# Memory branch: two heads share one score tile in 64-row halves, values in 64-column tiles, and TensorE's order is a fixed list

## The chip, the cores and the metric

The kernel runs on one core of one Trainium2 chip. The metric is the device time of one launch in microseconds (us); lower is better. Before the change it is 3423.18 us, the median of 2 runs (3422.0 to 3424.37).

## The reference

Two branches read the same input `x` (2048 rows, 640 columns) and are mixed by a gate for each row. Branch A is attention in a sliding window of 256 rows with 32 heads of 20 columns. Branch B goes through the rows in 64 segments of 32 and carries 8 memory rows from each segment to the next; it has 32 heads of 192 columns.

```python
    def _B_ref(x, mem0, Wq, Wk, Wv, Wo, seg_len):
        mask = (idx[:, None] < M) | (idx[:, None] >= idx[None, :])
        mem = mem0
        for s in range(n_seg):
            xs = x[:, s * seg_len:(s + 1) * seg_len, :].copy()
            h = jnp.concatenate([mem, xs], axis=1)
            q = jnp.einsum('btd,dhe->bhte', h, Wq)
            k = jnp.einsum('btd,dhe->bhte', h, Wk)
            v = jnp.einsum('btd,dhe->bhte', h, Wv)
            scores = jnp.einsum('bhqe,bhke->bhqk', q, k) * scale
            scores = jnp.where(mask[None, None], scores, -1000000000.0)
            p = _softmax(scores, axis=-1)
            o = jnp.einsum('bhqk,bhke->bhqe', p, v)
            o = jnp.einsum('bhte,hed->btd', o, Wo)
            mem = o[:, :M, :].copy()
            outs.append(o[:, M:, :])
    ...
    g = _sigmoid((x * gate_w).sum(-1, keepdims=True))
    return g * a + (1 - g) * b
```

So segment s + 1 cannot begin before the output projection of segment s has ended.

## The kernel before

The program has three stages. Branch A (up to about 560 us) also sets a part of branch B's weights into SBUF. Then `load_resident` brings the rest, and `tail_projections` computes q, k and v of the last 8 rows of every segment, which depend on `x` alone, and stores them in HBM (`xbqk`, `xbv`). From about 770 us on, `branch_B` runs its 64 segments one after the other.

A segment's `hT` holds 8 memory rows and the first 24 of the segment's 32 rows, transposed; the other 8 rows come from the stored tail. Its 40 rows (`L`) are worked on in 4 groups of 8 heads. For each group there are these steps:

- `chunk` for q, k and v: 20 matmuls in four column tiles of 32 (`tile_position=(0, 32 * j)`), the contraction over 640 in five passes (L556); ACT evicts the result (L560).
- `turn` of q and k: three transposes (L569), evicted into `QT` (ACT, L586), `K02` (DVE, L598) and `Kz` (ACT, two halves, L602); POOL adds the tail's columns (L590, L606, L608).
- `scores`: 12 matmuls into one bank, 40 rows by 8 heads times 40 columns (L624 to L627). `Kz` holds the middle third of the 192 columns of two heads, padded with zeros.
- softmax on 40 partitions by 320 elements: scale and mask (L634), maximum, subtraction, exp on ACT (L645), sum, reciprocal, and two multiplications into `Pm` and `Px` (L661, L667).
- the turn of the probabilities (L675, L677) and their spreading with a 0/1 mask into `PTm` and `PTx` (DVE, L682, L686).
- `pv`: seven matmuls into two banks (L702 to L711), evicted into `OT` by three ACT copies (L718, L722).
- `oproj`: 60 matmuls a group, which add to one bank over all four groups (L736).

At the segment's end DVE copies the new memory rows into the next `hT` (L755), ACT copies the output, TensorE turns it (L767), DVE mixes it with branch A's part (L773), and POOL's queue stores it.

Of the 64 weight tiles of 480 KB, 46 stay in SBUF. The other 18 (`STREAMED`) are fetched again in each segment from a packed copy in HBM, through a ring of four buffers, by DMAs on SP's queue (L390). A fetch waits until TensorE is done with the tile that had its buffer before.

The order of the work comes from `Sched`. Every step is an operation with an engine, an estimated length, and the buffers that it reads and writes. `run` walks through a model of the engines, takes on each the ready operation with the longest remaining chain, and emits all of them in the order of the modelled start times. The fetches of weights are not operations there; they are issued inside the chunk or projection that needs them:

```python
    LAT = {"PE": 200, "DVE": 60, "ACT": 60, "POOL": 100, "DMA": 2000}
...
            o = max((o for o in ready[eng] if at[o["n"]] <= t0), key=lambda o: o["rank"])
...
            ws = [weights.get(ring, kind, 4 * g + j) for j in range(4)]
```

## Time and profile before

| | before |
|---|---|
| median of the runs | 3423.18 us |
| the profiled execution | 3421.99 us, of which the span is 3420.3 us |
| TensorE busy | 2606.8 us (76%), 46613 matmuls |
| VectorE, ScalarE, GpSimd busy | 1498.6 us (44%), 1427.6 us (42%), 511.3 us (15%) |
| mean granted TensorE clock | 0.843 |
| DMA | 668.35 MB, mean 195 GB/s |

The busy shares are means over three stages with different limits. In the segments the rows of one stage recur 64 times, so a period and what fills it say more than the shares. In the page and in the answers about the trace, PE is TensorE's matmuls, PEld its weight loads, DVE VectorE, ACT ScalarE, POOL GpSimd, SP the queue of SyncE. [...] "w_ring" is a streamed weight tile.

### The profile page before, as it was taken

How to read it: one execution, taken by the hardware profiler on the slowest of the kernel's cores; microseconds unless marked ns; L12 is line 12 of the kernel's file. 1: busy time of each engine (PE TensorE's matmuls, PEld its weight loads, DVE VectorE, ACT ScalarE, POOL GpSimd, SP SyncE). 2: the span in 40 equal slices, each digit the busy share in tenths (PEclk: the TensorE clock that was granted, in tenths of full speed). 3: DMA queues.
4: the chain of work that ended last, by engine and by line, in shares of the span. 5: the costliest groups of instructions: out<-in, count | busy, mean ns of one | idle time of the engine just before them, and what ended most of it. 6: DMA issues, size and time to landing. Idle time of an engine off the chain costs nothing.

```text
span 3420.3 us, 107679 instructions
## 1 busy us (share of the span) xinstructions
PE 2606.8 (76%) x46613; PEld 1845.1 (54%) x46613; DVE 1498.6 (44%) x3834; ACT 1427.6 (42%) x3713; POOL 511.3 (15%) x1616
## 2 busy tenths in 40 slices
PE   6988886887777777777777777777777777777776
PEld 5777775754544444544545555445545455554554
DVE  6777773323333333333434433333433334343333
ACT  5878774223333333333333333333333333333333
POOL 6100000001111111111111111111111111111111
PEclk9989898898888888878889888878888888888887
DMA  8100004966667666666677666766666666666665
GB/s 261 56 19 14 20 10 127 175 152 221 225 230 233 231 222 219 224 217 226 229 229 242 226 224 223 237 219 228 230 219 226 218 229 229 228 235 224 223 229 187
DMA packets 303244, 668.35 MB, mean 195 GB/s; under 512 B 123656, under 2 KB 140048, under 8 KB 302768
## 3 DMA queue, kind: packets, MB, share of 16 engines
q1 hardware_dynamic: 282272, 613.24, 56.0%
q0 software_dynamic: 19840, 47.41, 4.3%
q8 instruction: 364, 5.96, 0.7%
q14 instruction: 112, 0.92, 0.1%
q10 hardware_dynamic: 656, 0.82, 0.1%
HBM read 634.60 MB, written 35.59 MB: 196 GB/s over the span
## 4 chain that ended last, share of the span: by engine, by line
PE 46%; DMA 21%; DVE 15%; ACT 11%; issue 5%; SPq 1%; POOL 0%; ACTq 0%; DVEq 0%; POOLq 0%
DMA w_ring<-w_packed 19%; PE ps_q L556 8%; PE ps_o L736 7%; PE ps_k L556 6%; PE ps_v L556 5%; ACT a_ex L195 3%; PE t_psum L416 3%; PE S_ps L624 2%; DVE t_PTx L686 2%; ACT a_pt L205 2%; DVE sm_sum L649 2%; ACT b_Kz L602 2%; DVE b_Pm L661 2%; PE ps_pv L702 1%; DVE t_PTm L682 1%
## 5 line engine op out<-in xcount | busy, mean ns | idle before, releaser
L556 PEld LDWEIGHTS <-t_hT 128*32 128x32 bf16 x15360 | 425.2, 107 | 564.5 <-issue 391.4
L556 PE MATMUL ps_v<-w_ring,t_hT 128*32 128x384 bf16 x1920 | 327.5, 359 | 187.9 <-DMA w_ring<-w_packed 187.7
L736 PEld LDWEIGHTS <-w_o 128*128 128x128 bf16 x11520 | 363.5, 100 | 125.9 <-issue 123.2
L736 PE MATMUL ps_o<-t_OT,w_o 128*128 128x40 bf16 x11520 | 400.4, 186 | 16.5 <-ACT t_OT L718 2.3
L634 DVE SCALAR_TENSOR_TENSOR S_ps<-S_ps,bmask 40x320 f32<-40x320 f32 x256 | 125.9, 492 | 535.1 <-PE S_ps L627 535.1
L556 PE MATMUL ps_q<-w_q,t_hT 128*32 128x384 bf16 x3840 | 328.0, 396 | 18.7 <-DVE t_hT L755 18.4
L556 PE MATMUL ps_v<-w_v,t_hT 128*32 128x384 bf16 x3200 | 331.5, 359 | 0.0
L556 PE MATMUL ps_q<-w_ring,t_hT 128*32 128x384 bf16 x1280 | 322.3, 395 | 5.7 <-DMA w_ring<-w_packed 5.5
L195 ACT ACTIVATE a_ex<-s_ps,a_nmx 128x384 bf16<-128x384 f32 (+2 forms) x512 | 288.6, 613 | 77.9 <-DVE a_nmx L193 77.5
L556 PE MATMUL ps_k<-w_k,t_hT 128*32 128x384 bf16 x3840 | 303.5, 373 | 0.0
L556 PE MATMUL ps_k<-w_ring,t_hT 128*32 128x384 bf16 x1280 | 299.9, 373 | 0.5 <-DMA w_ring<-w_packed 0.5
L602 ACT COPY b_Kz<-tr_k 64x128 bf16<-64x128 bf16 x512 | 132.7, 259 | 384.8 <-DVE t_K L598 372.5
L560 ACT CAST t_vtok<-ps_v 128x384 bf16<-128x384 f32 x256 | 122.4, 478 | 374.4 <-PE ps_v L556 373.1
L193 DVE TENSOR_REDUCE a_nmx<-s_ps 128x1 f32<-128x384 f32 (+2 forms) x512 | 252.8, 524 | 27.3 <-PE s_ps L190 22.0
L606 POOL COPY t_K<-t_xqk 128x64 bf16<-128x64 bf16 x256 | 60.3, 236 | 1282.6 <-PE S_ps L627 1281.9
L560 ACT CAST t_tok<-ps_q 128x384 bf16<-128x384 f32 x256 | 122.4, 478 | 272.6 <-PE ps_q L556 272.6
L682 DVE TENSOR_TENSOR t_PTm<-PT_ps,mk_m 128x320 bf16<-128x320 f32 x256 | 125.9, 492 | 250.8 <-PE PT_ps L677 250.8
L675 PE MATMUL PT_ps<-ident,b_Pm 128*128 128x40 bf16 x512 | 55.3, 186 | 224.5 <-DVE b_Pm L661 224.5
L649 DVE TENSOR_REDUCE sm_sum<-S_ps 40x8 f32<-40x320 f32 x256 | 123.6, 483 | 219.4 <-ACT S_ps L645 219.4
L702 PE MATMUL ps_pv<-t_PTx,b_xv 128*128 128x320 bf16 x256 | 90.7, 354 | 148.5 <-DVE t_PTx L686 148.2
L718 ACT CAST t_OT<-ps_pv 128x320 bf16<-128x320 f32 x256 | 108.8, 425 | 217.4 <-PE ps_pv L705 212.8
L202 PE MATMUL pt_ps<-a_ident,a_ex 128*128 128x128 bf16 x1440 | 160.5, 219 | 42.9 <-ACT a_pt L205 25.9
(144 smaller groups left out, 5753.9 us busy)
## 6 DMA issues: line engine op xcount, KB each, us to landing
w_ring<-w_packed SPq DMA_DIRECT2D x1166, 480.0 KB, 4.8
xbqk<-t_qk SPq DMA_DIRECT2D x16, 768.0 KB, 7.0
t_xqk<-xbqk POOLq DMA_DIRECT2D x64, 192.0 KB, 4.5
xbv<-t_vt SPq DMA_DIRECT2D x64, 96.0 KB, 1.9
b_xv<-xbv POOLq DMA_DIRECT2D x128, 48.0 KB, 2.9
w_q<-in_B_Wq_dram POOLq DMA_DIRECT2D x12, 480.0 KB, 8.8
w_k<-in_B_Wk_dram POOLq DMA_DIRECT2D x12, 480.0 KB, 8.0
w_v<-in_B_Wv_dram SPq DMA_DIRECT2D x10, 480.0 KB, 7.8
```

The costliest lines, as they stand in the source:

```text
L193: nc.vector.tensor_reduce(out=nmx[:], in_=sp[:, 0:nk * P], axis=AX.X, op=ALU.max, negate=True)
L195: nc.scalar.activation(out=ex[:, 0:nk * P], in_=sp[:, 0:nk * P], func=ACT.Exp, bias=nmx[:], scale=1.0)
L202: nc.tensor.transpose(pt_ps[:, ci, :], ex[:, ci * P:(ci + 1) * P], ident[:])
L556: nc.tensor.matmul(t[32 * j:32 * j + 32, 0:384], lhsT=tile_of(hT)[:, kt, :], rhs=ws[j][:, kt, :], start=(kt == 0), stop=(kt == KT - 1), ti ...
L560: sc.op("ACT", act(384), lambda: nc.scalar.copy(tile_of(tok)[:], b["tile"][:, 0:384]), reads=[b], writes=[tok])
L602: nc.scalar.copy(tile_of(Kz)[64 * r:64 * r + 64, :, r, 0:SEG], src)
L634: nc.vector.scalar_tensor_tensor(out=view(), in0=view(), scalar=scale, in1=mask[:].unsqueeze(1).to_broadcast([L, 8, L]), op0=ALU.mult, op1 ...
L649: nc.vector.tensor_reduce(out=x["sum"][:], in_=view(), axis=AX.X, op=ALU.add)
L682: nc.vector.tensor_tensor(out=tile_of(PTm)[:], in0=PT["tile"][:, 0:2, :].unsqueeze(2).to_broadcast([P, 2, 4, L]), in1=mk_m[:].unsqueeze(1) ...
L702: nc.tensor.matmul(t0[:, 0:320], lhsT=xvt[:, off:off + P], rhs=x[:].rearrange("p a j l -> p (a j l)"), start=True, stop=False, skip_group_ ...
L718: nc.scalar.copy(dst[:, 0:2, :, :], o0["tile"][:, 0:320].rearrange("p (a j l) -> p a j l", a=2, l=L))
L736: nc.tensor.matmul(t[:, dt * L:(dt + 1) * L], lhsT=w[:, b, dt * P:(dt + 1) * P], rhs=OT["tile"][:, 3 * i + b, :], start=(g == 0 and i == 0 ...
```

## The change

In branch B, without a change to what is computed:

- Scores of a group go into a tile of 128 partitions and 160 columns: head a of each pair in partitions 64a to 64a + 39. 18 matmuls on two column tiles of 64 (`tile_position=(0, 64 * a)`); the first two write the mask, so the pass of L634 is gone, and the scale goes into the exp. The softmax works on 160 elements.
- `Kz` is written by one DVE multiplication with a 0/1 mask instead of two ACT copies. `QT`, `K02`, `Kz`, `PTm` and `PTx` have two buffers instead of one.
- Values are 12 matmuls on two column tiles of 64 in one bank, and one ACT copy evicts them. For that the rows of Wo are laid out anew in their weight tile: two DMAs a tile instead of four.
- The probabilities are turned by two matmuls instead of three, in steps (`turn_p`) that stand by themselves in the order.
- The 16 steps of the output projection become four, of 60 matmuls each.
- TensorE's order is given by the text `STEP` for one segment, repeated; `x` is the turn of the previous segment's output. The model still sets the order on the other engines. Fetches of weights are operations of it, on SP, and the model's lengths and latencies are new.

What this does to the order on three engines follows. First ScalarE at the border of two segments, around the copy of the output into `b_oT`. `t_tok<-ps_q` is the eviction of a q chunk, `t_vtok<-ps_v` of a v chunk, `b_QT` that of a turned q, `S_ps<-S_ps` the exp, `t_OT` the values. Before:

```order
L722 CAST t_OT<-ps_pv_39135 64x4x40 x2
L760 CAST b_oT_14573<-ps_o 128x160
L560 CAST t_tok<-ps_q 128x384
L560 CAST t_tok<-ps_k 128x384
L586 COPY b_QT_14559<-tr_q 128x3x4x32
L560 CAST t_tok<-ps_q 128x384
L560 CAST t_tok<-ps_k 128x384
L602 COPY b_Kz_14561<-tr_k 64x4x32 x2
L560 CAST t_vtok<-ps_v 128x384
L586 COPY b_QT_14559<-tr_q 128x3x4x32
L560 CAST t_tok<-ps_q 128x384
L645 ACTIVATE S_ps<-S_ps 40x320
```

After:

```order
L609 CAST t_vtok<-ps_v 128x384
L749 CAST t_OT<-ps_pv 128x480
L609 CAST t_vtok<-ps_v 128x384 x2
L749 CAST t_OT<-ps_pv 128x480 x2
L782 CAST b_oT_14546<-ps_o 128x160
L609 CAST t_tok<-ps_k 128x384
L609 CAST t_tok<-ps_q 128x384
L609 CAST t_tok<-ps_k 128x384
L628 COPY b_QT_14530<-tr_q 128x3x4x32
L609 CAST t_tok<-ps_q 128x384 x2
L628 COPY b_QT_14531<-tr_q 128x3x4x32
L689 ACTIVATE S_ps<-S_ps 128x160
```

Before, q chunks come first in a segment, three of them with two k chunks, two turned q and a v chunk ahead of the first exp. Now k comes first, the v chunk is gone from there, and the eviction of the values, one copy for a group instead of two or three, stands twice behind the last two v chunks of the segment before.

Second, VectorE on two of the four groups (`sm_mx`, `sm_sum`, `sm_rs` are maximum, sum and reciprocal). Before, one group:

```order
L634 SCALAR_TENSOR_TENSOR S_ps<-S_ps,bmask 40x320
L639 TENSOR_REDUCE sm_mx<-S_ps 40x8
L642 TENSOR_TENSOR S_ps<-S_ps,sm_mx 40x320
L649 TENSOR_REDUCE sm_sum<-S_ps 40x8
L653 RECIPROCAL sm_rs<-sm_sum 40x8
L661 TENSOR_TENSOR b_Pm_14564<-S_ps,sm_rs 40x256
L667 TENSOR_TENSOR b_Px_14568<-S_ps,sm_rs 40x64
L682 TENSOR_TENSOR t_PTm<-PT_ps,mk_m 128x320
L686 TENSOR_TENSOR t_PTx<-PT_ps,mk_x 128x320
```

After:

```order
L727 TENSOR_TENSOR t_PTx<-PT_ps,mk_x 128x320
L727 TENSOR_TENSOR t_PTm<-PT_ps,mk_m 128x320
L683 TENSOR_REDUCE sm_mx<-S_ps 128x4
L693 TENSOR_REDUCE sm_sum<-S_ps 128x4
L686 TENSOR_TENSOR S_ps<-S_ps,sm_mx 128x160
L697 RECIPROCAL sm_rs<-sm_sum 128x4
L704 TENSOR_TENSOR t_Pm<-S_ps,sm_rs 128x128
L708 TENSOR_TENSOR b_Px_14540<-S_ps,sm_rs 128x32
L693 TENSOR_REDUCE sm_sum<-S_ps 128x4
L697 RECIPROCAL sm_rs<-sm_sum 128x4
L704 TENSOR_TENSOR t_Pm<-S_ps,sm_rs 128x128
L708 TENSOR_TENSOR b_Px_14541<-S_ps,sm_rs 128x32
```

The pass with `bmask` is gone, passes have 128 partitions and half as many elements, and passes of two groups alternate. The spreads into `t_PTm` and `t_PTx` no longer follow their own group's `b_Px` at once.

Third, TensorE at a group's scores (`b_QT` is q turned, `t_K` and `b_Kz` are parts of k). Before, one of the group's four head pairs:

```order
L624 LDWEIGHTS b_QT_14559
L624 MATMUL S_ps<-b_Kz_14561,b_QT_14559 128x80
L626 LDWEIGHTS b_QT_14559
L626 MATMUL S_ps<-t_K_21450,b_QT_14559 128x40
L627 LDWEIGHTS b_QT_14559
L627 MATMUL S_ps<-t_K_21450,b_QT_14559 128x40
```

After, the mask and the first pair:

```order
L666 LDWEIGHTS ident
L666 MATMUL S_ps<-bmask,ident 64x160
L666 LDWEIGHTS ident
L666 MATMUL S_ps<-bmask,ident 64x160
L673 LDWEIGHTS b_QT_14530
L673 MATMUL S_ps<-t_K_40305,b_QT_14530 64x40
L673 LDWEIGHTS b_QT_14530
L673 MATMUL S_ps<-t_K_40305,b_QT_14530 64x40
L673 LDWEIGHTS b_QT_14530
L673 MATMUL S_ps<-b_Kz_14534,b_QT_14530 64x40
L673 LDWEIGHTS b_QT_14530
L673 MATMUL S_ps<-b_Kz_14534,b_QT_14530 64x40
```

Each matmul is half as wide (64 columns of the array), a pair takes four of them instead of three, and two with the mask stand ahead: 18 instead of 12 in all.

The diff, cut to its core:

```diff
-    LAT = {"PE": 200, "DVE": 60, "ACT": 60, "POOL": 100, "DMA": 2000}
+
+    LAT = {"PE": 190, "DVE": 125, "ACT": 140, "POOL": 150, "DMA": 2000, "SP": 2000}
+    SWITCH = 100
...
-    def run(self):
+    def run(self, names=None, emit=True):
         ops = self.ops
+        if names is not None:
+            named = {o["name"]: o for o in ops if o["eng"] == "PE"}
+            assert len(named) == len(names) == sum(o["eng"] == "PE" for o in ops)
+            names = [named[n] for n in names]
...
+                if eng == "PE" and names is not None:
+                    rs = [o for o in rs if o is names[k]] if k < len(names) else []
...
+            if eng == "PE" and names is not None:
+                o = names[k]
+                k += 1
+            else:
+                o = max((o for o in ready[eng] if at[o["n"]] <= t0), key=lambda o: o["rank"])
             ready[eng].remove(o)
-            at[o["n"]] = t0
+            if eng == "PE":
+                if mode is not None and o["mode"] != mode:
+                    t0 += self.SWITCH
+                mode = o["mode"]
...
-            engine.dma_start(dst[:, a, :], self.Wo[2 * pr + a, 0:128, :])
-            engine.dma_start(dst[64 * a:64 * a + 64, 2, :], self.Wo[2 * pr + a, 128:192, :])
+            engine.dma_start(dst[64 * a:64 * a + 64, :, :], self.Wo[2 * pr + a].rearrange("(b p) e -> p b e", p=64))
...
+def pe_order(nseg):
+
+    out = []
+    for s in range(nseg):
+        for w in STEP.split():
+            d = 1 if w[0] == "x" else 0
+            if s - d >= 0:
+                out.append((w[:-1] if w[-1].isdigit() else w, s - d) + ((int(w[-1]),) if w[-1].isdigit() else ()))
+    out.append(("x", nseg - 1))
+    return out
+
+
+STEP = "k0 q0 tk0 k1 tq0 x q1 q2 s0 tk1 tq1 k3 k2 s1 tq2 tk2 q3 p0 tk3 s2 v0 tq3 p1 pv0 s3 v1 o0 p2 pv1 p3 v2 v3 pv2 o1 pv3 o2 o3"
...
-    ring = ctx.enter_context(tc.tile_pool(name="b_ring", bufs=4))
     sb = {
-        "hT": (2, [P, KT, SEG]), "tok": (3, [P, 384]), "vtok": (2, [P, 384]), "K02": (1, [P, 4, 2, L]),
-        "PTm": (1, [P, 2, 4, L]), "PTx": (1, [P, 2, 4, L]), "OT": (2, [P, 12, L]),
-        "xqk": (1, [P, 4, 2, 12, MEM]), "ga": (1, [SEG, D]), "res": (1, [SEG, D]),
+        "w": (4, [P, 1920]), "hT": (2, [P, KT, SEG]), "tok": (3, [P, 384]), "vtok": (2, [P, 384]), "K02": (2, [P, 4, 2, L]),
+        "PTm": (2, [P, 2, 4, L]), "PTx": (2, [P, 2, 4, L]), "OT": (2, [P, 3, 4, L]), "Pm": (2, [P, 4, SEG]),
+        "xqk": (1, [P, 4, 2, 12, MEM]), "xv": (1, [P, 384]), "ga": (1, [SEG, D]),
...
-        return 155 + n / 0.96
+        return 75 + n / 0.96
 
     def act(n):
-        return 152 + n / 1.2
-
-    def load_x(hb, s):
+        return 60 + n / 1.2
...
+    def load_w(kind, pr):
+        if (kind, pr) not in weights.slot:
+            return None
+        b = sc.buf("w")
+        sc.op("SP", 1250, lambda: nc.sync.dma_start(tile_of(b)[:], weights.packed[weights.slot[kind, pr]]), writes=[b])
+        return b
...
+        wb = [load_w(kind, 4 * g + j) for j in range(4)]
...
-        sc.op("PE", 850, f, reads=[hT], writes=[b])
+        sc.op("PE", 800, f, reads=[hT] + [w for w in wb if w], writes=[b], name=(kind, s, g), mode=32)
...
+        def ev_z():
+            src = tk["tile"][:, 1, :].rearrange("p (j t) -> p j t", t=SEG).unsqueeze(2).to_broadcast([P, 4, 2, SEG])
+            nc.vector.tensor_tensor(out=tile_of(Kz)[:, :, :, 0:SEG], in0=src,
+                                    in1=mk_z[:].unsqueeze(1).unsqueeze(3).to_broadcast([P, 4, 2, SEG]), op=ALU.mult)
...
+    def scores(s, g):
+        QT, (K02, Kz) = made.pop(("Q", s, g)), made.pop(("K", s, g))
+        S = sc.buf("s")
+
+        def f():
+            t = tile_of(S, [P, 512], FP32, "S_ps")
             for a in range(2):
+                nc.tensor.matmul(t[64 * a:64 * a + 64, 0:4 * L], lhsT=ident[:, 64 * a:64 * a + 64],
+                                 rhs=mask[:].rearrange("p j l -> p (j l)"), start=True, stop=False,
+                                 tile_position=(0, 64 * a), skip_group_check=True)
+            for j in range(4):
+                for b in range(2):
+                    for a in range(2):
+                        c = (3 * j + (1 if b else 2 * a)) * L
+                        nc.tensor.matmul(t[64 * a:64 * a + 64, j * L:(j + 1) * L], lhsT=QT["tile"][:, c:c + 64],
+                                         rhs=(Kz if b else K02)["tile"][:, j, a, :], start=False, stop=(b == 1),
+                                         tile_position=(0, 64 * a), skip_group_check=True)
+        o = sc.op("PE", 400, f, reads=[QT, K02, Kz], writes=[S], name=("s", s, g), mode=64)
+        view = lambda: S["tile"][:, 0:4 * L].rearrange("p (j l) -> p j l", l=L)
+        wide = lambda t, n: t[:].unsqueeze(2).to_broadcast([P, 4, n])
...
+            nc.scalar.activation(out=view(), in_=view(), func=ACT.Exp, scale=scale)
...
+        for eng, dur, f in (("DVE", dve(160), f1), ("DVE", dve(160), f2), ("ACT", act(160), f3), ("DVE", dve(160), f4), ("DVE", dve(4), f5)):
+            o = sc.op(eng, dur, f, reads=[S], after=[o])
...
+    def turn_p(s, g):
+        Pm, Px = made.pop(("P", s, g))
+        PT = sc.buf("tr")
+
+        def f():
+            t = tile_of(PT, [P, 2, 2, L], FP32, "PT_ps")
+            rhs = ident[:].rearrange("p (a c) -> p a c", c=64)[:, :, 0:L]
+            nc.tensor.matmul(t[:, 0, :, :], lhsT=Pm["tile"][:].rearrange("p j t -> p (j t)"), rhs=rhs, start=True, stop=True)
+            nc.tensor.matmul(t[:, 1, :, :], lhsT=Px["tile"][:], rhs=rhs, start=True, stop=True)
+        sc.op("PE", 90, f, reads=[Pm, Px], writes=[PT], name=("p", s, g), mode=128)
+        PTm, PTx = sc.buf("PTm"), sc.buf("PTx")
+
+        def spread(i, dst, mk):
+            nc.vector.tensor_tensor(out=tile_of(dst)[:], in0=PT["tile"][:, i, :, :].unsqueeze(2).to_broadcast([P, 2, 4, L]),
+                                    in1=mk[:].unsqueeze(1).unsqueeze(3).to_broadcast([P, 2, 4, L]), op=ALU.mult)
+        sc.op("DVE", dve(320), lambda: spread(1, PTx, mk_x), reads=[PT], writes=[PTx])
+        sc.op("DVE", dve(320), lambda: spread(0, PTm, mk_m), reads=[PT], writes=[PTm])
+        made["PT", s, g] = (PTm, PTx)
+
+    def values(s, g):
+        PTm, PTx = made.pop(("PT", s, g))
+        V, xv = made.pop(("v", s, g)), tails[s][1]
+        o = sc.buf("mm")
+
+        def f():
+            t = tile_of(o, [P, 512], FP32, "ps_pv")
+            for b in range(3):
+                for i, (p, v) in enumerate(((PTx, tile_of(xv)), (PTm, V["tile"]))):
+                    for a in range(2):
+                        c = 192 * a + 64 * b
+                        nc.tensor.matmul(t[64 * a:64 * a + 64, 160 * b:160 * b + 160], lhsT=v[:, c:c + 64],
+                                         rhs=p["tile"][:, a, :, :].rearrange("p j l -> p (j l)"), start=(b == 0 and i == 0),
+                                         stop=(i == 1), tile_position=(0, 64 * a), skip_group_check=True)
+        sc.op("PE", 430, f, reads=[PTm, PTx, V, xv], writes=[o], name=("pv", s, g), mode=64)
+        OT = sc.buf("OT")
+        sc.op("ACT", act(480), lambda: nc.scalar.copy(tile_of(OT)[:].rearrange("p b j l -> p (b j l)"), o["tile"][:, 0:480]),
+              reads=[o], writes=[OT])
+        made["O", s, g] = OT
...
+        sc.op("PE", 60 * 25.4, f, reads=[OT] + [w for w in wb if w], writes=[o_b], name=("o", s, g), mode=128)
...
+        return sc.run([("m0", 0)] + names)
```

362 lines of the change are left out of this document (148 added, 214 removed).

## The prediction

> **What bounds the kernel now.** I read the page first: one engine does not fill the chain of work that ended last.
>
> ```profile
> PE 46%; DMA 21%; DVE 15%; ACT 11%; issue 5%; SPq 1%; POOL 0%; ACTq 0%; DVEq 0%; POOLq 0%
> ```
>
> Nearly all of the span is the 64 segments of the memory branch, which depend on each other through the copy of the new memory into `hT` (L755). The listing of that line dates them.
>
> ```profile
> L755 DVE CAST t_hT<-ps_o x63: 198/200/201, 814.6 to 3371.4; 128x40 bf16<-128x40 f32 x63
> ```
>
> 63 copies make 62 periods: (3371.4 − 814.6)/62 = 41.24 us a segment. Everything below is a sum for one segment. The chain, in order of time, through one of them (start, length, what):
>
> ```profile
> 2028.75 0.85 PE ps_o L736 x30
> 2029.61 0.93 PE ps_q L556 x20
> 2030.53 0.48 PE ps_o L736 x15
> ...
> 2032.30 0.27 ACT b_Kz L602
> ...
> 2032.89 0.20 PE S_ps L624
> ...
> 2033.39 0.17 PE tr_q L569 x3
> 2033.56 0.96 PE ps_k L556 x20
> 2034.53 4.37 DMA w_ring<-w_packed
> ...
> 2041.28 0.50 DVE S_ps L634
> 2041.80 0.49 DVE sm_mx L639
> 2042.32 0.50 DVE S_ps L642
> 2042.90 0.41 ACT S_ps L645
> 2043.34 0.49 DVE sm_sum L649
> 2043.85 0.20 DVE sm_rs L653
> 2044.08 0.43 DVE b_Pm L661
> ...
> 2045.33 0.49 DVE t_PTx L686
> 2045.86 0.43 PE ps_pv L702
> ...
> 2047.12 0.28 ACT t_OT L722
> ...
> 2047.76 1.84 PE ps_o L736 x50
> 2049.62 0.21 DVE t_hT L755
> ...
> 2049.87 1.79 PE ps_q L556 x16
> ```
>
> Two things stop TensorE. It waits for streamed weights (4.37 us), and the softmax of the last head group (2041.28 to 2044.51, 3.23 us) has little beside it. The PE timeline and the DMA view of 1500 to 2300 us, and the time to landing of the ring's transfers, price the transfers:
>
> ```profile
> 2015.77 0.32 PE L556 MATMUL ps_v<-w_ring,t_hT 128*32 128x384 bf16 x1 [1.17 <-DMA w_ring<-w_packed]
> ...
> 2016.98 0.32 PE L556 MATMUL ps_v<-w_ring,t_hT 128*32 128x384 bf16 x1 [0.87 <-DMA w_ring<-w_packed]
> ```
>
> ```profile
> DMA packets 54859, 181.74 MB, mean 227 GB/s; under 512 B 7490, under 2 KB 7490, under 8 KB 54743
> ...
> q1 hardware_dynamic: 50327, 171.77, 64.5%
> q0 software_dynamic: 4416, 8.28, 3.3%
> ```
>
> ```profile
> DMA to landing us min/median/max: 3.1/4.8/8.4
> ```
>
> Two landings in a full queue are 1.21 us apart; one alone takes some 3.5 us (my estimate between the 3.1 and the 4.8). Now the third loss, in windows of 3.41 us (length, PE busy, granted clock, DMA share, GB/s):
>
> ```profile
> 2014.20:2017.61 3.41, 1.38 (x22) 1.00 1.00 332
> 2017.61:2021.03 3.42, 3.24 (x44) 0.50 0.86 303
> 2021.03:2024.44 3.41, 0.69 (x8) 1.00 0.74 250
> 2024.44:2027.85 3.41, 3.41 (x46) 0.50 0.01 2
> 2027.85:2031.26 3.41, 3.41 (x106) 1.00 0.68 200
> ...
> 2041.50:2044.92 3.42, 1.83 (x57) 1.00 0.98 372
> ```
>
> A window in which TensorE was busy for 0.69 or 1.38 us is followed by one at clock 0.50; a full one by one at 1.00. At 0.50 a q chunk takes 1.79 us instead of 0.93. So every long wait is paid again in the next window, and the DMA queue then runs empty (share 0.01). [...]
>
> **The change, part by part.** *TensorE's own work at full clock.* The two `ps_o` rows give (0.85 − 0.48)/15 = 24.7 ns a matmul and 0.11 us fixed, which I take as the price of changing the tile form. Per segment: 12 chunks at 0.95 = 11.4; o-projection 4 × (60 × 0.0247 + 0.11) = 6.4; 8 turns at 0.17 = 1.4, in 6 runs with 0.11 each = 0.7; five transposes of the store at a turn's 0.17/3 = 0.057, 0.3; probability turns 4 × 2 × 0.057 = 0.4.
>
> Scores go from 12 matmuls (2032.89 to 2033.39, 0.50 us) to 18 on half-width tiles. Nothing in the trace runs that form. The nearest is the chunk, 20 matmuls on 32-column tiles, four beside each other. If pairs overlap likewise, 18 cost what 9 to 12 do, 0.38 to 0.50; if they follow one another at the chunk's 0.84/20 = 42 ns, 0.76. I take 0.50 + 0.11: 4 × 0.61 = 2.4. Values, warm:
>
> ```profile
> 2032.07 0.31 PE L702 MATMUL ps_pv<-t_PTx,b_xv 128*128 128x320 bf16 x1 [0.43 <-DVE t_PTx L686]
> ...
> 2032.56 0.23 PE L711 MATMUL ps_pv<-t_PTm,t_vtok 128*128 128x160 bf16 x1
> ```
>
> That is 0.72 us for 1280 columns, 0.56 ns each. The new form streams 12 × 160; in pairs 960 columns are left, 0.54 us, and one after another 1920, 1.08. I take 0.6 + 0.11: 2.8. Form changes, counted in the order, rise from 16 to 25 a segment (their 0.11 are in these terms). Sum 25.8, and from the last `ps_o` to the first chunk of the next segment 0.25 (2049.62 to 2049.87): 26.0 us.
>
> [...]
>
> *The softmax.* One group now holds its 8 heads on two halves of the partitions, 160 elements instead of 320, and the mask pass (0.50) is gone into TensorE.
>
> ```profile
> L667 DVE TENSOR_TENSOR b_Px<-S_ps,sm_rs 40x64 bf16<-40x64 f32 x78 | 16.0, 205 | 0.0
> ```
>
> From 64 elements (0.205) and 320 (0.50) follow 0.32 for 160 and 0.28 for 128. The chain becomes 3 × 0.32 + exp 0.28 + 0.20 + 0.28 + gaps 0.25 = 2.0 us instead of 3.23. Its cover in the new order: between s3 and p3 stand v1, o0, p2, pv1 (3.4 us), between s0 and p0 4.8. The same holds for the spreads of p3 (2 × 0.49): v2, v3, pv2, o1. So this wait goes to zero; without cover it would cost up to 2 us a group. `Kz` moves from two ACT copies (0.27 each) to one DVE pass of 256 elements, at most the 0.49 of the spreads' 320; the values' eviction from three ACT copies to one of 480 elements, at most 3 × 0.28. DVE then holds, a group, 1.44 of softmax, 0.17 for `Px`, 0.98 of spreads and under 0.9 for K: 14 us of 26 a segment, and ACT has fewer instructions than now. Both have room: no cost. The mask needs two of the 18 matmuls, counted above.
>
> *The weights.* Still 18 transfers in a ring of four, 9.37 MB a segment with the rest (181.74 × 41.24/800). At the fullest window's 372 GB/s that is 25.2 us: nearly TensorE's 26.0. So what matters is whether each lands in time. Time 0 is the end of o3. Its slot takes q1's weights: landed at 3.5, while k0, q0, tk0, k1, tq0, x hold TensorE until 4.0. k0's slot, free at 1.2, takes q2's: 4.7, wanted 4.95. v0's second, in k3's slot (free 8.0): 11.5, wanted 11.8. v2's two, in v0's slots (12.75): 17.5 at worst, wanted 18.0; v3's, from v1's (15.4): 18.9, wanted 19.0. Margins of 0.1 to 0.5 us. Transfers 0.3 later than I assume cost about 1.2 us over these places; none costs nothing. I add 0.6: **26.6 us a segment**. SP holds nothing but these transfers there. POOL's stores and loads stand in a row too: `out` waits for the DVE pass at about 6, and only the K copies for s2 (wanted at 11) are behind it.
>
> *Ahead of the segments.* The resident Wo loads become 2 issues a unit instead of 4.
>
> ```profile
> 574.70 1.45 SPq L374 DMA_DIRECT2D w_o<-in_B_Wo_dram  x1
> ...
> 605.27 0.47 SPq L375 DMA_DIRECT2D w_o<-in_B_Wo_dram  x1
> ```
>
> 48 issues take 31 us of SP, and TensorE's tail projection waits behind them. With half the issues but the same rows, bounds are 0 (the bytes set the pace) and −15; I take −10.
>
> **The sum.** The profiled execution took 3421.99 us (median of the two 3423.18, so a microsecond apart). 64 × (41.24 − 26.6) = 937. 3422 − 937 − 10 = **2475 us**.
>
> **Rivals.**
> *Transfers set the pace* (0.18). The queue's 64.5% of 800 us over 349 transfers is 1.48 us each, above the 1.21; all queues' share comes to 28.3 us a segment. If the engines really need that, the period is 28.3 + 0.7 of ring empty at the boundary = 29.0: 3422 − 64 × 12.24 − 10 = 2629. Against it: 1.21 between landings, and 372 GB/s.
> *The 64-column tiles do not pair* (0.10). Scores +0.26, values +0.48 a group: period 29.6, time 2667. Against it: chunk matmuls on tiles do overlap.
> *The order holds only in its model* (0.06). One late link (a DVE pass behind another group's, a K copy behind a store) makes TensorE, which can no longer go round it, stand for 1 us or more in many places; the clock then falls in some windows. Periods of 30 to 38, 2690 to 3200.
> *Slower* (0.02): the clock stays at half. If short waits are spread so that each 3.41 us window has TensorE busy for under some 1.8 us, all work is paid at 0.50: chunks 12 × 1.79 = 21.5, o-projection 240 × 0.037 (1.84 for 50) = 8.9, the other 8.0 doubled to 16.0, and the boundary: 46.7 us, 3422 + 64 × 5.5 − 10 = 3764. From 26.6 at full clock it decides once four fifths of the time is at half (26.6 + 0.8 × 20 = 42.7, 2% over now). For it speaks that every wait of 2 us has this price now; against it that TensorE would be busy over 95% by the sum.
> *No change by 2%* (0.02): the waits only move.
>
> **How the numbers follow.** My forecast has 0.62, with 25.2 to 28 us a segment: 2385 to 2564. The range adds the first two rivals and the mildest of the third: 2385 to 2690 (period 30), which leaves out the rest and a part of each, some 2 in 10. Some 2% is what a measurement here can tell: faster 0.96, same 0.02, slower 0.02.
>
> **What would show it.** The copy into `hT` every 26 to 27 us. Clock above 0.95 in the segments. DMA over 330 GB/s. Chain mostly TensorE, the softmax lines almost gone from it, and each weight wait under 0.5 us. Scores from first to last near 0.5 us, values near 0.6. The forecast is wrong if landings in a full queue are 1.4 us apart, if scores take 0.75 us or more, or if the clock stays near 0.83.

## The result, and the profile after

The changed kernel took 2766.68 us (median of two runs, 2763.76 to 2769.6) beside 3423.18 us: 0.8082 of the time, with a 95% interval of 0.8044 to 0.8121. The forecast was 2475 us and its range ended at 2690: the side was right, the size was not. The profiled execution took 2769.6 us, with a span of 2767.9.

The listing of the line that copies the new memory into `hT`, in the kernel after (count, duration in ns, first and last start):

```profile
L777 DVE CAST t_hT<-ps_o x63: 199/200/201, 804.2 to 2732.3; 128x40 bf16<-128x40 f32 x63
```

(2732.3 − 804.2)/62 = 31.10 us a segment, where 26.6 were forecast and 41.24 stood before. 64 × (41.24 − 31.10) = 649 us, nearly the whole of the 652 us between the two profiled executions.

The kernel after, chain that ended last, shares of the span by engine:

```profile
DMA 40%; PE 30%; issue 2%; DVE 0%; POOL 0%; SPq 0%; POOLq 0%; ACT 0%; ACTq 0%; DVEq 0%
```

DVE and ACT, 15% and 11% of the chain before, are gone from it; DMA has doubled from 21% to 40%. What the softmax held up is now held up by weights. One stretch of this chain, in order of time (start, length, what):

```profile
1521.83 4.86 DMA t_w<-w_packed
...
1526.73 0.97 PE ps_v L605 x17
...
1530.13 5.67 DMA t_w<-w_packed
...
1535.85 0.99 PE ps_v L605 x19
1536.84 0.54 PE ps_pv L744 x12
1537.38 1.62 PE ps_o L768 x60
1539.01 5.72 DMA t_w<-w_packed
```

A chunk ends, frees a slot, the next transfer into that slot takes 5 to 6 us, and the chunk that wants it begins when it lands: the chain goes round through the ring. No DVE or ACT work stands in this stretch of the chain.

The same kernel from 1500 to 2300 us, by the windows (length, busy time of PE, PEld, DVE, ACT and POOL, granted clock, DMA share, GB/s):

```profile
1500.00:2300.00 800.00, 676.76 (x16269) 460.50 (x16271) 306.27 (x1061) 277.62 (x633) 167.48 (x561) 0.98 0.88 298
```

by the DMA view (packets, MB and share of the engines' time for the queues; for the transfers count, size, and median us to landing):

```profile
q1 hardware_dynamic: 66016, 225.34, 83.0%
...
q8 instruction: 127, 2.08, 1.0%
...
t_w<-w_packed SPq DMA_DIRECT2D x458, 480.0 KB, 5.3
```

and by the waits (us in total, times, longest):

```profile
PE ps_v L605 <- DMA t_w<-w_packed: 64.0, 87, 2.6
PE ps_q L605 <- DMA t_w<-w_packed: 33.6, 42, 1.8
...
PE ps_k L605 <- DMA t_w<-w_packed: 5.4, 12, 1.5
...
PEld L768 <- DMA t_w<-w_packed: 4.0, 7, 1.4
...
PE ps_o L768 <- DMA t_w<-w_packed: 3.2, 6, 1.3
```

These 800 us are 25.7 segments, so TensorE waits 110.2/25.7 = 4.3 us a segment for weights in plain sight, in 154/25.7 = 6.0 waits. That is less than the waits cost. The view counts idle time from the end of the last row, and a row of a chunk lasts 0.33 us while the next matmul starts some 0.04 us after the last (the prediction's 0.84/20). By an estimate from these figures each wait costs 0.3 us more, 1.8 a segment. The clock is 0.98 although the waits are many: they last 110.2/154 = 0.7 us on the average. The DMA engines are not full either: they work for 0.88 of the time and move 298 GB/s.

### The profile page after: what moved, and what is told of

Read it like the earlier page. It is cut to its first block, busy times and chain, and to the rows that moved or that the text cites. A ratio compares the mean times of both kernels' runs of the same rounds, so it can differ in the third digit from the quotient of the medians.

```text
span 2767.9 us, 112051 instructions
## 1 busy us (share of the span) xinstructions
PE 2334.9 (84%) x49157; PEld 1678.4 (61%) x49173; DVE 1229.7 (44%) x3835; ACT 1161.4 (42%) x2689; POOL 509.0 (18%) x1611
## 4 chain that ended last, share of the span: by engine, by line
DMA 40%; PE 30%; issue 2%; DVE 0%; POOL 0%; SPq 0%; POOLq 0%; ACT 0%; ACTq 0%; DVEq 0%
DMA t_w<-w_packed 40%; PE ps_o L768 8%; PE ps_v L605 7%; PE ps_k L605 5%; PE ps_q L605 4%; PE ps_pv L744 3%; PE S_ps L673 1%; PE tr_q L619 1%; PE tr_k L619 1%; PE S_ps L666 1%; DVE t_hT L777 0%; PE ox_ps L793 0%; PE PT_ps L721 0%; PE PT_ps L722 0%; DMA xbv<-t_vt 0%
## 5 line engine op out<-in xcount | busy, mean ns | idle before, releaser
L605 PE MATMUL ps_v<-t_w,t_hT 128*32 128x384 bf16 x1920 | 300.5, 336 | 152.9 <-DMA t_w<-w_packed 148.5
L605 PE MATMUL ps_q<-t_w,t_hT 128*32 128x384 bf16 x1280 | 253.1, 329 | 68.1 <-DMA t_w<-w_packed 65.9
L605 PE MATMUL ps_k<-t_w,t_hT 128*32 128x384 bf16 x1280 | 255.1, 331 | 21.7 <-DMA t_w<-w_packed 17.2
L193 DVE TENSOR_REDUCE a_nmx<-s_ps 128x1 f32<-128x384 f32 (+2 forms) x512 | 253.3, 524 | 27.2 <-PE s_ps L190 22.0
L749 ACT CAST t_OT<-ps_pv 128x480 bf16<-128x480 f32 x256 | 143.2, 559 | 216.5 <-PE ps_pv L744 213.1
L609 ACT CAST t_tok<-ps_k 128x384 bf16<-128x384 f32 x256 | 122.7, 479 | 203.6 <-PE ps_k L605 203.6
L187 PE MATMUL s_ps<-KT_blk,QTm 128*128 128x128 bf16 x1440 | 191.4, 226 | 3.5 <-DVE KT_blk L134 2.7
L205 ACT COPY a_pt<-pt_ps 128x384 bf16<-128x384 bf16 (+2 forms) x352 | 175.5, 509 | 15.8 <-PE pt_ps L202 14.0
L683 DVE TENSOR_REDUCE sm_mx<-S_ps 128x4 f32<-128x160 f32 x256 | 82.5, 322 | 220.1 <-PE S_ps L673 220.1
L727 DVE TENSOR_TENSOR t_PTx<-PT_ps,mk_x 128x320 bf16<-128x320 f32 x256 | 125.2, 489 | 110.8 <-PE PT_ps L722 110.5
L642 DVE COPY t_K<-tr_k 128x256 bf16<-128x256 bf16 x256 | 72.2, 282 | 224.7 <-PE tr_k L619 224.5
```

The lines of the kernel that those rows point to most:

```text
L187: nc.tensor.matmul(sp[:, ci * P:(ci + 1) * P], lhsT=qm[r][:, g, :], rhs=kring[c][:, g, :], start=True, stop=not need_mask)
L193: nc.vector.tensor_reduce(out=nmx[:], in_=sp[:, 0:nk * P], axis=AX.X, op=ALU.max, negate=True)
L205: nc.scalar.copy(pt[:, 0:nk, :], pt_ps[:, 0:nk, :])
L605: nc.tensor.matmul(t[32 * j:32 * j + 32, 0:384], lhsT=tile_of(hT)[:, kt, :], rhs=ws[j][:, kt, :], start=(kt == 0), stop=(kt == KT - 1), ti ...
L609: sc.op("ACT", act(384), lambda: nc.scalar.copy(tile_of(tok)[:], b["tile"][:, 0:384]), reads=[b], writes=[tok])
L683: nc.vector.tensor_reduce(out=x["mx"][:], in_=view(), axis=AX.X, op=ALU.max)
```

## The experiments

Each run has one profiled execution, and all but the last two rest on a single execution (the kernel before took 3422.05 us beside the first four, 3427.34 beside the next four, and 3424.47, the median of seven, beside the last four). Periods are (last − first start)/62 of the `hT` copy, unless said otherwise.

### What the fetches cost

**No fetches.** Every streamed weight is replaced by a resident one.

```diff
 def load_w(kind, pr):
-    if (kind, pr) not in weights.slot:
-        return None
+    return None
...
 def w_of(kind, pr, b):
+    if (kind, pr) in weights.slot:
+        pr = 4 * (pr // 4)
...
```

> No weight tile is fetched in the segments: each of the 18 streamed tiles is replaced by the first resident tile of its group, so the numbers are not the reference's. TensorE's work, order and everything else stay. Theory (the fetches alone make up the gap between the 26.6 us a segment of the prediction and the 31.1 measured): the period falls to 26.0 to 26.8, the kernel to 2440 to 2490 us, clock 0.97 or more. Rival (the fixed list itself, or the half-width tiles, cost more than the sum had): the period stays above 28.5, the kernel above 2600 us.

Measured: 2323.96 us. The `hT` copies of this run:

```profile
L778 DVE CAST t_hT<-ps_o x63: 198/199/201, 794.5 to 2292.1; 128x40 bf16<-128x40 f32 x63
```

24.15 us a segment, below the 26.0 to 26.8 that were expected; "the list or the half-width tiles cost more" (above 28.5) falls. Its window from 1200 to 2000 us, and some pieces of its chain:

```profile
1200.00:2000.00 800.00, 790.29 (x21128) 573.36 (x21125) 393.83 (x1386) 363.46 (x827) 216.65 (x729) 1.00 0.08 21
```

```profile
1503.20 0.19 PE S_ps L667 x2
1503.38 0.24 PE S_ps L674 x16
...
1515.50 0.54 PE ps_pv L745 x12
```

TensorE is busy for 99% of the time at full clock: this is the kernel's own work, and the prediction had 26.0 for it. Scores take 0.43 us (0.50 + 0.11 in the prediction), values 0.54 (0.6 + 0.11). The fetches cost the kernel 31.10 − 24.15 = 6.95 us a segment.

**The kernel before without fetches**, by the same edit in its `get`.

```diff
 u = (kind, pr)
+if u in self.slot:
+    u = (kind, 4 * (pr // 4))
 if u in self.tiles:
```

> The kernel before, with every streamed weight replaced by a resident one of the same group, so that nothing is fetched in the segments (the outputs are not the reference's). It prices the fetches of the kernel before, as the same edit of the kernel after priced its own (31.10 to 24.15 us a segment). Theory 'two losses': the kernel before lost about as much to the softmax chain as to fetches; without fetches its period falls from 41.24 to 31 to 35 us, and with full clock in most windows. Rival 'fetches were the loss': 26 to 29 us, nearly all of the 17 us between 41.24 and 24.15 lay in the weight waits and the half clock that they brought, and the new tiles and order have little part in the gain. Rival 'the chain was the loss': 37 us or more.

Measured: 3057.18 us. Its copies, and its window from 1500 to 2100 us:

```profile
L757 DVE CAST t_hT<-ps_o x63: 199/200/201, 793.6 to 3013.9; 128x40 bf16<-128x40 f32 x63
```

```profile
1500.00:2100.00 600.00, 479.40 (x9964) 331.22 (x9960) 272.09 (x701) 252.75 (x687) 110.18 (x369) 0.86 0.05 14
```

35.81 us, a little above the 31 to 35 of "two losses" and below the 37 of "the chain was the loss"; "fetches were the loss" falls. The kernel before lost only 5.43 us a segment to its fetches, and without them it still ran at clock 0.86 with TensorE busy for 80% of the time. So the parts of the change that are not fetches took 35.81 − 24.15 = 11.66 us off, and the fetches, pressed into a shorter segment, took 6.95 − 5.43 = 1.52 us back.

**Half the bytes.** The same transfers, each of the first half of the columns (the other half of the buffer, which is set to zero once at the start, stays zero).

```diff
...
-nc.sync.dma_start(tile_of(b)[:], weights.packed[...])
+nc.sync.dma_start(tile_of(b)[:, 0:960], weights.packed[...][:, 0:960])
```

> Each of the 18 fetches brings the first half of each row (240 KB instead of 480); the other half of the buffer stays zero, so the numbers are not the reference's. TensorE reads and waits as before. If the bytes set the pace, a fetch costs half and no longer holds TensorE up: the period falls to 26.5 to 27.5 us, the kernel to 2470 to 2540. If the time from issue to landing of a single fetch sets it (about 4.6 us when others are under way, of which only some 0.6 goes with the bytes), the period falls by no more than half of the excess: 28.8 to 30.5 us, 2620 to 2730.

Measured: 2350.69 us. Its copies, and its DMA view of 1200 to 2000 us:

```profile
L777 DVE CAST t_hT<-ps_o x63: 198/200/200, 796.0 to 2319.4; 128x40 bf16<-128x40 f32 x63
```

```profile
q1 hardware_dynamic: 84582, 144.38, 61.6%
...
b_w<-w_packed SPq DMA_DIRECT2D x589, 240.0 KB, 3.3
```

24.57 us, below both expectations (26.5 to 27.5, and 28.8 to 30.5): half the bytes took 2.0 us off the landing, not 0.6. Just as many transfers and issues cost 0.42 us a segment once they land in 3.3 us instead of 5.3. So it is how long a transfer of 480 KB takes that costs, not that it is issued or signalled.

**The fixed order taken out.** The planner's model chooses TensorE's order again; tiles, buffers and fetches stay.

```diff
-return sc.run([("m0", 0)] + names)
+return sc.run()
```

> The fixed list of TensorE's steps is dropped: the changed model, with its new lengths and with the fetches as operations, picks TensorE's order by the longest remaining chain, as before the change. All tiles, buffers and steps stay those of the changed kernel. If the list carries a large part of the gain, the period rises from 31.1 to 34 us or more (above 2950 us); if the tiles, the buffers and the model of the fetches carry it, it stays within 1.5 us of 31.1 (2670 to 2870).

Measured: 2835.85 us, with this row of copies:

```profile
L777 DVE CAST t_hT<-ps_o x63: 198/200/201, 805.1 to 2797.3; 128x40 bf16<-128x40 f32 x63
```

32.13 us, 1.03 more than with the list and within the 1.5 of "the tiles, the buffers and the model of the fetches carry it". The written order is worth some 2.5% here, where fetches hide a part of what an order can do.

### How fast the queue can be

**Unread fetches.** All transfers are issued as in the kernel after, but the matmuls read resident weights, so no chunk waits for a transfer and no slot waits for a chunk.

```diff
     sc.op("SP", 1250, lambda: nc.sync.dma_start(...), writes=[b])
-    return b
+    return None
...
 def w_of(kind, pr, b):
+    if (kind, pr) in weights.slot:
+        pr = 4 * (pr // 4)
...
```

> The 18 fetches of a segment are issued as before into the same ring of four, but no matmul reads them (the first resident tile of the group takes their place, the numbers are not the reference's), so that a fetch waits only for the one that had its buffer. This measures how fast the queue goes when nothing holds it up. If the DMA engines need 1.48 us for each tile (64.5% of 800 us over 349 tiles before the change), the 1152 fetches take about 1700 us; if a full queue lands one every 1.2 us, about 1390 us. In both cases TensorE's period is that of the kernel without fetches within 0.5 us, unless the traffic itself slows TensorE.

Measured: 2594.97 us. Its DMA view of 1200 to 2000 us:

```profile
DMA packets 85447, 284.01 MB, mean 355 GB/s; under 512 B 11453, under 2 KB 11453, under 8 KB 85279
...
q1 hardware_dynamic: 79039, 269.83, 92.2%
...
t_w<-w_packed SPq DMA_DIRECT2D x548, 480.0 KB, 5.8
```

800/548 = 1.46 us a transfer when nothing holds the queue up: 18 × 1.46 = 26.3 us a segment, already more than TensorE's 24.15. The 1152 transfers were issued from 752.7 to 2432.0 us, in 1679 us: near the 1700 of the expectation, not the 1390. The prediction's 1.21 us between two landings and its 372 GB/s were moments; 355 GB/s is what lasts, with the DMA engines busy for 0.98 of the time. What sets that rate, the engines or something behind them, the run does not tell.

The second finding was not expected. TensorE waits for no weight here, and yet the copies, in the stretch with the stream and then after the stream had ended, show it slower:

```profile
L779 DVE CAST t_hT<-ps_o x48: 198/200/200, 1026.3 to 2385.4; 128x40 bf16<-128x40 f32 x48
```

```profile
L779 DVE CAST t_hT<-ps_o x6: 199/200/200, 2442.9 to 2563.7; 128x40 bf16<-128x40 f32 x6
```

(2385.4 − 1026.3)/47 = 28.92 us with the stream, (2563.7 − 2442.9)/5 = 24.16 without. The chain of this run shows where the 4.8 us are ("issue" is time in which the engine waited for nothing that the profile shows):

```profile
1516.43 0.83 PE ps_k L607 x16
1517.27 2.37 issue
1519.64 0.35 PE ps_k L607 x4
...
1545.40 0.83 PE ps_k L607 x16
1546.23 2.66 issue
```

TensorE stops after the 16th of the 20 matmuls of a chunk, all of whose operands are there, and does so again at the same matmul of the next segment. A place in the program, not a piece of data, is late; that speaks for the instructions themselves. The trace has a DMA queue of that name: in the kernel after, "instruction" moves 2.08 MB in 127 packets, 16 KB each, from 1500 to 2300 us. The table below counts the gaps of TensorE of over 0.8 us between 1200 and 2000 us of a trace, and those of them that ended 1.1 to 1.6 us after a packet of 16 KB had landed. In this run that is so for 49 of 50 gaps, where chance would give 9%. The runs with a ring of five are told of below; the 57 gaps of the kernel after are nearly all waits for weights.

```
                                gaps   end 1.1 to 1.6 us after a 16 KB packet
no fetches                         0     0
unread fetches, ring of four      50    49
unread fetches, ring of two        5     5
the kernel after                  57     2
ring of five, 19 streamed         44    20
ring of five, 18 streamed         45    29
the same kernel, second profile   45    20
```

**Unread fetches in a ring of two**, to tell the late instructions from a price on bytes. The edit is that of the unread fetches, and this:

```diff
-"w": (4, [P, 1920])
+"w": (2, [P, 1920])
```

> The unread fetches again (the matmuls read resident weights of the same group, so the outputs are not the reference's), but in a ring of two: two transfers under way instead of four. It asks what slows TensorE in a full queue (28.9 us a segment instead of 24.15, with no weight to wait for). Theory 'the instructions wait behind the transfers': each gap of TensorE ends some 1.3 us after a packet of 16 KB of the instruction queue; with half as many packets ahead of it the instructions come in time, and the period while the stream lasts falls to 24.2 to 25.5 us, although the queue still moves 230 to 300 GB/s. Rival 'traffic slows TensorE by its bytes': the loss goes with GB/s; at 260 instead of 355 the period is 24.15 + 4.75 x 260/355 = 27.6 us.

Measured: 3319.28 us, which is no time of TensorE's: the unread stream itself went on until 3312 us. The copies, and the DMA view of 1200 to 2000 us:

```profile
L779 DVE CAST t_hT<-ps_o x63: 198/200/200, 800.9 to 2332.1; 128x40 bf16<-128x40 f32 x63
```

```profile
DMA packets 57690, 187.99 MB, mean 235 GB/s; under 512 B 8686, under 2 KB 8686, under 8 KB 57499
...
t_w<-w_packed SPq DMA_DIRECT2D x349, 480.0 KB, 4.5
```

24.70 us a segment at 235 GB/s. A price in proportion to the bytes would have made it 24.15 + 4.77 × 235/355 = 27.3. With two transfers under way TensorE loses 0.55 us, with four 4.77: in these two runs the loss goes with how full the queue is. The edit changes two things together, the transfers under way and the share of time in which the DMA engines work (0.77 instead of 0.98), so which of these makes the instructions late is not shown. The gaps over 0.8 us sum to 79.9 us in the 27.7 segments of the unread run, 2.9 us of the 4.77; the other 1.9 (shorter gaps, and a clock of 0.96 instead of 1.00) were not traced further.

### How deep the ring must be

Three kernels change the number of slots, and pay for it with weights made resident or streamed, or with buffers.

**Five slots, 19 streamed.**

```diff
-"w": (4, [P, 1920])
+"w": (5, [P, 1920])
...
-"o": {0: (3,), 1: (3,), 2: (3,), 3: (3,)}
+"o": {0: (3,), 1: (1, 3), 2: (3,), 3: (3,)}
```

> A ring of five instead of four, paid for with one more streamed weight (19 a segment instead of 18). Theory 'depth': a slot of the ring takes 31.10 x 4/18 = 6.9 us round, landing 5.2 of it; four slots keep the queue busy 0.88 of the time, five fill it, and 19 x 1.46 = 27.7 us becomes the bound: period 28 to 29.8, time 2570 to 2690. Rival 'bytes at any depth': the queue's share stays near 0.88 and one more transfer costs another 1.5 to 1.8 us: period 32.5 to 33, time 2860 to 2890. Rival 'TensorE under traffic': with a fuller queue TensorE loses as much to the traffic as it wins at the waits: 30 to 31.5.

**Five slots, 18 streamed.** The room comes from the buffers that the change had doubled, and the order is shifted where a single buffer asks for it.

```diff
-"w": (4, ...), "K02": (2, ...), "PTm": (2, ...), "PTx": (2, ...), "QT": (2, ...), "Kz": (2, ...)
+"w": (5, ...), "K02": (1, ...), "PTm": (1, ...), "PTx": (1, ...), "QT": (1, ...), "Kz": (1, ...)
...
-p0 tk3 s2 v0 tq3 p1 pv0 s3 v1 o0 p2 pv1 p3 v2 v3 pv2 o1
+p0 s2 tk3 v0 tq3 pv0 p1 s3 v1 o0 pv1 p2 v2 v3 pv2 p3 o1
```

> A ring of five with the same 18 streamed weights; the room comes from single instead of double buffers for the q rows, both K tiles and both spread probability tiles, and the fixed order is shifted at four places so that it still can run. Theory 'depth': 18 x 1.46 = 26.3 us is the bound, but the unread fetches showed TensorE at 28.9 us under a full queue: period 28 to 29.5, time 2570 to 2670, unless the single buffers cost more than 1 us. Rival 'bytes at any depth': 31 us or more. Against the ring of five with 19 it prices the nineteenth transfer: 'bytes bind' makes it 1.46 us dearer, 'TensorE under traffic' makes the two equal.

**Three slots, 17 streamed.**

```diff
-"w": (4, [P, 1920])
+"w": (3, [P, 1920])
...
-"v": {0: (1, 3), 1: (1,), 2: (1, 3), 3: (1,)}
+"v": {0: (1, 3), 1: (1,), 2: (1,), 3: (1,)}
```

> A ring of three, with one weight more resident (17 a segment). Theory 'depth': three slots of 6.4 to 6.9 us (landing gets shorter in a queue that is less full) make 17/3 x 6.4 to 6.9 = 36 to 39 us, time 3080 to 3270, with the queue's share at 0.70 or less. Rival 'bytes at any depth': 17/18 of 31.1 = 29.4 us, time 2660.

Measured: 2673.18, 2656.63 and 2924.13 us. The copies of the three, in this order:

```profile
L777 DVE CAST t_hT<-ps_o x63: 199/200/200, 799.3 to 2637.3; 128x40 bf16<-128x40 f32 x63
```

```profile
L777 DVE CAST t_hT<-ps_o x63: 199/200/201, 796.8 to 2620.4; 128x40 bf16<-128x40 f32 x63
```

```profile
L777 DVE CAST t_hT<-ps_o x63: 199/200/200, 806.4 to 2883.1; 128x40 bf16<-128x40 f32 x63
```

and the transfers of 1500 to 2300 us:

```profile
t_w<-w_packed SPq DMA_DIRECT2D x515, 480.0 KB, 5.8
```

```profile
t_w<-w_packed SPq DMA_DIRECT2D x495, 480.0 KB, 5.6
```

```profile
t_w<-w_packed SPq DMA_DIRECT2D x407, 480.0 KB, 4.5
```

The time that a slot takes to go round is the period times the slots, over the transfers of a segment:

| slots, streamed | period, us | a slot's round, us | median to landing, us |
|---|---|---|---|
| 3, 17 | 33.50 | 5.9 | 4.5 |
| 4, 18 | 31.10 | 6.9 | 5.3 |
| 5, 19 | 29.65 | 7.8 | 5.8 |
| 5, 18 | 29.41 | 8.2 | 5.6 |

The expectations of the two kernels with five slots held in their numbers (28 to 29.8, and 28 to 29.5 us). "Bytes at any depth" falls twice: one transfer fewer with a slot less made the kernel slower, one more with a slot more made it faster. For three slots "depth" had the right side but 36 to 39 us; the queue, less full (the DMA engines worked for 0.82 of the time instead of 0.88), landed its transfers in 4.5 us, earlier than assumed. With three and four slots 1.4 and 1.6 us of a round are not landing, and the chunk that reads the slot takes 0.95 of them: there the ring is the limit. With five slots 2.0 and 2.6 us are left. The gaps say the same. Of those over 0.8 us (1200 to 2000 us), 65 of 65 with three slots and 54 of 57 with four are waits for weights, with five 26 of 44 (19 streamed) and 7 of 45 (18 streamed). Some waits of this last kernel (1500 to 2300 us):

```profile
PE S_ps L673 <- POOL b_QT L632: 19.5, 24, 1.4
PE ps_q L605 <- issue: 19.4, 17, 2.7
PE ps_v L605 <- issue: 19.1, 15, 2.3
...
PE ps_v L605 <- DMA t_w<-w_packed: 14.0, 20, 1.9
...
PE ps_q L605 <- DMA t_w<-w_packed: 2.2, 3, 1.5
...
PE ps_k L605 <- DMA t_w<-w_packed: 1.9, 8, 0.3
```

The waits for weights are 18.1 us in 27.2 segments, 0.7 a segment instead of 4.3. But the period fell by 1.7 us only, for two other waits have grown. TensorE waits 0.7 us a segment for `b_QT`, the turned q to which POOL adds the tail's columns; with 19 streamed, where `b_QT` keeps two buffers, that wait is 0.6 us in all. What makes POOL late was not followed up. And 43.1 us, 1.6 a segment, are waits for nothing that the profile shows ("issue": the two rows above, and 4.6 us at other steps); in the kernel after the like is 7.2 us, 0.3 a segment. In the table of gaps all 20 of this kind end with an instruction packet (19 of 20 in the second profile of the same kernel, 16 of 16 with 19 streamed). The rest of the 29 are 9 of the 18 gaps that wait for `b_QT`, of which the second profile has only 1 of 15.

The kernel with 19 streamed is slower by 0.24 us, not by 1.46. The two differ in more than the transfer, though: the single buffers and the shifted order cost the other one 0.36 us without fetches (next run) and, with them, the 0.7 for `b_QT`. So a nineteenth transfer costs 0.6 to 1.3 us by an estimate from these rows. The DMA engines work for 0.94 and 0.92 of the time there, against 0.98 in the unread run: the queue is nearly full, not full.

**Five slots without fetches**, to see what the single buffers cost. It is the kernel with five slots and 18 streamed under the edit of "no fetches"; the ring, declared with four slots here, is not used.

> The ring-of-five kernel (18 streamed, single buffers, shifted order) with all fetches replaced by resident weights (outputs not the reference's). It splits its 29.41 us. Theory 'the single buffers cost little': 24.15 to 24.8 us a segment, and the other 4.6 to 5.2 us are the traffic, as with the unread fetches (4.75). Rival 'the single buffers cost what is left': 26 us or more.

Measured: 2350.16 us.

```profile
L778 DVE CAST t_hT<-ps_o x63: 198/200/200, 798.7 to 2318.4; 128x40 bf16<-128x40 f32 x63
```

24.51 us: the single buffers and the shifted order cost 0.36. The other 29.41 − 24.51 = 4.9 us come with the fetches. That is close to the 4.77 of the unread fetches, but not made up alike: 0.7 of it are waits for weights, and 0.7 the wait for `b_QT`, which this run does not have and the unread one for 0.6 us in all.

**Five slots timed, and the streamed weights spread.** The second kernel streams the same number, but no chunk waits for two fetches.

```diff
-"v": {0: (1, 3), 1: (1,), 2: (1, 3), 3: (1,)}, "o": {0: (3,), 1: (3,), 2: (3,), 3: (3,)}
+"v": {0: (1,), 1: (1,), 2: (1,), 3: (1,)}, "o": {0: (1, 3), 1: (3,), 2: (1, 3), 3: (3,)}
```

> The ring-of-five kernel with 18 streamed weights once more, timed: its one look gave 2656.6, against 2766.7 of the changed kernel. If the depth of the ring is worth 1.7 us a segment, 2650 to 2665.

> The same ring of five and 18 streamed weights, but which units are streamed is changed: the v chunks of groups 0 and 2 have one instead of two, the o-projections of groups 0 and 2 two instead of one. Theory 'lumps': two fetches that one chunk waits for come 1.4 us apart, so the v chunks hold the last waits for weights (8 us in 600, 0.33 us a segment): 29.0 to 29.3 us a segment, 2630 to 2650. Rival 'the queue is full, only traffic is left': within 0.5% of the kernel of run e11.

Measured: 2661.29 us (four runs, 2652.04 to 2664.69), 0.7769 of the kernel before (0.7745 to 0.7794); spread 2642.78 us (2636.38 to 2652.58), 0.7720 (0.7688 to 0.7753). The waits for weights of the spread kernel, 1500 to 2300 us:

```profile
PE ps_k L605 <- DMA t_w<-w_packed: 22.4, 28, 1.9
...
PE ps_v L605 <- DMA t_w<-w_packed: 0.5, 1, 0.5
```

The waits left the v chunks and went to the k chunks. They did not shrink: with 0.6 us at the q chunks they are 23.5 us, 0.86 a segment, where the timed kernel has 20.7 us, 0.76. So "lumps" was wrong in its mechanism. The medians differ by 0.7%, but the intervals overlap and the periods (29.48 and 29.32 in the two profiles) differ by 0.16 us, so whether spreading is worth anything stays open. That both beat the changed kernel does not: 0.772/0.8082 = 0.955 of its time.

## Why the prediction was right or wrong

**The step that failed is the walk of the transfers.** It took "one alone takes some 3.5 us" to landing, added 1.21 us for each more in line, and found margins of 0.1 to 0.5 us at five places, so an allowance of 0.6 us; the fetches cost 6.95. In the kernel after the median to landing is 5.3 us, 1.8 more than assumed and more than any of those margins. Where the time went shows from the start of each step to the start of the next. The table has means over segments between 1000 and 2200 us of which every matmul is on record, 49 without fetches and 37 of the kernel after:

| step | no fetches, us | after, us | more |
|---|---|---|---|
| q1 | 0.82 | 0.94 | 0.12 |
| q2 | 0.92 | 1.59 | 0.67 |
| v0 | 0.93 | 2.45 | 1.52 |
| v2 | 0.82 | 2.19 | 1.37 |
| v3 | 0.92 | 1.61 | 0.69 |
| q0 | 0.92 | 2.04 | 1.12 |
| the four k chunks | 3.49 | 4.41 | 0.92 |
| the four o-projections | 6.34 | 6.64 | 0.30 |
| first matmul to the copy into `hT` | 23.90 | 30.87 | 6.97 |

The first five are the walk's places: 4.4 us where it allowed 0.6. Another 1.12 us were lost at q0 and 0.92 at the k chunks, for which it names no margin. The 3.5 was chosen between the row's minimum of 3.1 and its median of 4.8, for a queue that the same text expected to be nearly full. That was the wrong end: the medians of these runs are 4.5 us at 265 GB/s, 5.3 at 298 and 5.8 at 355. The warning stood there ("transfers 0.3 later than I assume cost about 1.2 us"), but the range went only as far as 30 us. Two of the prediction's signs failed with it: more than 330 GB/s (298) and waits for weights under 0.5 us (0.7 on the average).

**The rival "transfers set the pace" was the mechanism in part.** It had 0.18 and 29.0 us a segment. It was right that 1.21 between two landings is no rate and that 1.48 is nearer to it (1.46 in the unread run). But the queue never became the limit at that rate: the DMA engines worked for 0.88 of the time, because four slots could not keep them full, and 31.10 lay above the rival too. No case of the prediction held the round of a slot.

**TensorE's own work was put too high:** 26.0 us against 24.15. Scores and values make 4 × (0.18 + 0.17) = 1.4 of the 1.85: the rows show no 0.11 for the change of form beside them, and scores on 64-column tiles took 0.43, below the 0.50 of the old form. This error hid a part of the other: −1.85 + (6.95 − 0.60) = +4.50, which is 31.10 − 26.6. The rival "64-column tiles do not pair" is refuted: it had 0.76 us for the scores of a group and 1.08 for its values, and the rows show 0.43 and 0.54.

**The softmax** went out of the chain as forecast: DVE and ACT stand at 0% of it, and with no fetches TensorE is busy for 99% of the time, which leaves no room for a wait there. That the order would hold was right as well: without fetches TensorE never stood for 0.8 us between 1200 and 2000 us. Without the list 1.03 us were lost.

**The clock** was forecast above 0.95 in the segments and was 0.98. "Slower: the clock stays at half" did not happen, but the reason given against it did not hold either: TensorE was to be busy for over 95% of the time and was for 85% (676.76 of 800 us), which was still enough. What the prediction did not see is how much of the old time was clock: without any fetch the kernel before still ran at 0.86. Of TensorE's 120.6 idle us in the 600 of its window, 105.4 were waits for VectorE's probabilities and their spreads, so most of the idle time beside that clock came from its softmax. How idle time and clock go together, the kernel before shows in the windows of the prediction (length, PE busy, granted clock, DMA share, GB/s):

```profile
2038.09:2041.50 3.41, 2.29 (x58) 1.00 0.87 275
2041.50:2044.92 3.42, 1.83 (x57) 1.00 0.98 372
2044.92:2048.33 3.41, 2.29 (x35) 0.50 0.28 102
```

After 2.29 us of work in 3.41 the clock was still 1.00, after 1.83 it was 0.50. That the softmax's waits did the same in the run without fetches is an inference from this; no row of that run shows it.

**The resident Wo loads** were to give 10 us and gave none. The issues, and the first matmul of the segments, in the kernel after:

```profile
L395 SPq DMA_DIRECT2D w_o<-in_B_Wo_dram x24: 595/596/1482, 575.1 to 601.7; - x24
```

```profile
L605 PE MATMUL ps_k<-w_k,t_hT x3840: 322/326/528, 772.0 to 2742.3; 128*32 128x384 bf16 x192
```

Half the issues took 0.6 us each and ended at 602.3 instead of 605.7; the segments began at 772.0 instead of 772.5. The bound of 0 was the right one. That the bytes set the pace is not shown by a run; it fits that the DMA engines were busy throughout 560 to 700 us in both kernels (a share of 0.99 before, no less after).

Put together: 2475 + 64 × 4.50 + 10 = 2773 us, and 2769.6 were measured.

## What to carry to other kernels

A ring of weights has a rate of its own, slots over the time of one round (landing plus holding; here four slots over 6.9 us, 5.3 of them landing); work it out from the median to landing in the fullest stretch of the trace, not from the gap between two landings, and compare it with the rate of the queue and of the engine before summing anything. Walk through every place that waits for a slot, not only those that look tight. When an edit shortens the work, transfers that were hidden are pressed together and can land later (here 18 in 31.10 us instead of 41.24, with a median to landing of 5.3 us instead of 4.9 in 1500 to 2300 us), so price them at the load that the edit brings. And when waits for data are gone and an engine still stops at the same place of the program each time round, look at the queue that brings its instructions (here 49 of 50 such gaps ended 1.1 to 1.6 us after one of its packets).
